# Branch hints, a shorter last wait, a split check and two PSUM banks at the end of a two-block attention kernel

## Chip, cores, metric

The kernel runs on one core of one Trainium2 chip. The metric is the device time of that core in microseconds (us). One execution of each kernel was also recorded by the profiler. Its "span" runs from the first to the last record and is about 1.8 us shorter than the device time of the same execution (853.9 beside 855.72 before the change).

## The reference, cut to what matters

Two cached attention blocks on the same shapes, written side by side into one output of 16 x 32 x 2048. Block A has 32 query heads on 4 K/V heads, block B has 32 K/V heads.

```python
# B = 16 batches, Sq = 32 queries, D = 1024, Sk = 1024 keys, Dh = 128, all bf16
def _A_ref(x, k_cache, v_cache, wq, wo):            # k_cache, v_cache: B x 4 x Sk x Dh
    q = (x @ wq).reshape(B, Sq, 32, Dh).transpose(0, 2, 1, 3)
    k, v = jnp.repeat(k_cache, 8, axis=1), jnp.repeat(v_cache, 8, axis=1)
    p = softmax(einsum("bhqd,bhkd->bhqk", q, k) * Dh ** -0.5)
    o = einsum("bhqk,bhkd->bhqd", p, v)
    return o.transpose(0, 2, 1, 3).reshape(B, Sq, 32 * Dh) @ wo
# _B_ref: the same without the repeat; k_cache, v_cache: B x 32 x Sk x Dh
return jnp.concatenate([a, b], axis=-1)
```

The traffic is almost all loads: 337.6 MB read, of which the K and V of block B are 268 MB, and 2.1 MB written.

## The kernel before, cut to what the argument touches

The kernel holds two programs. The fast one takes exponentials without subtracting a row maximum. It notes every reciprocal of a softmax sum and at its end checks that all lie between 1e-10 and 1e10; the answer becomes a number in SBUF, the flag. The second, "general", program is safe for all inputs and follows behind a branch on that flag. With the inputs of this case the flag is always good, so the branch always jumps over the general program.

```python
def run_engine(self, eng_name, eng, sems):
    for op in self.ops:                      # the engine's own instructions, in scheduled order
        ...
def await_dmas(self, eng, sems):
    for k, c in sorted(self.dma_count.items()):     # all 40 DMA semaphores, two to an instruction
        eng.wait_ge(sems[k], 16 * c)

def whole(name, eng):                        # written once for each of the five engines
    fast.run_engine(name, eng, fast_sems)
    eng.wait_ge(fast_sems[flag_op.eng], flag_op.sig)
    reg = eng.alloc_register("flag_" + name)
    eng.reg_load(reg, flag[0:1, 0:1])
    if name == "sp":
        fast.await_dmas(eng, fast_sems)      # before the branch
    with eng.If_ne(reg, flag_good):
        ...                                  # the general program
```

The fast program is a list of operations with what each reads and writes. A list scheduler orders the operations of all engines by modelled times and adds the semaphores, so a small edit can move instructions far from it. It runs 128 steps. Each step does four heads of one batch of B (a "quad") and a part of A. Tokens come in four groups of 128 (G = 0 to 3). At the end of each group's block the output projection adds into `acc`; in the last block it goes to the staging buffer `ost` and from there to the output:

```python
def oproj(pi, blk, G):                       # pi: 0 for A, 1 for B
    for oh in range(NOH):                    # two halves of 512 columns
        for h0_ in range(0, nh, 2):
            ...                              # matmuls into ps_pj, one PSUM bank for both halves
        a_ap = acc[:, pi, G, oh * OUTW:(oh + 1) * OUTW]
        o_ap = ost[:, oh * OUTW:(oh + 1) * OUTW]
        ...
        else:                                # last block
            pr.add("dve", lambda e: e.tensor_tensor(o_ap, a_ap, ps_pj[:, 0:OUTW], ALU.add),
                   reads=[BK_PJ, ("acc", pi, G, oh)], writes=[BK_PJ, "ost"], name="accF")
    if blk == nblk - 1:                      # one store of 128 x 1024 bf16, 256 KB
        pr.add("sp", lambda e: e.dma_start(out_flat[...], ost[:, :]), reads=["ost"], dma_key=f"out{pi}")

def st_check():                              # the last thing in the program
    # DVE: two scans over all 2*128 reciprocals -> good[P, 2]   (>= 1e-10, <= 1e10)
    # PE:  ones x good -> ps_pj[0, 0:2];  DVE: multiply, multiply, cast -> flag
```

A "PV" below is the product of the probabilities of one quad with V: 32 matmuls. After it come, for each quad, a normalization (DVE), a transpose (PE) and a copy (ACT), and after the last quad of a group the output projection of B.

Of the kernel before, what the change touches and what calls it, by code (L numbers as in the profile page):

```python
# [7 lines left out]
ALU = alu_op_type.AluOpType  # L8
ACTF = mybir.ActivationFunctionType
BF = mybir.dt.bfloat16  # L10
F32 = mybir.dt.float32


RINV_LOW, RINV_HIGH = 1e-10, 1e10
NVB_SLOTS = 3
NKB_SLOTS = 2
LAZY_PER_STEP = 100
LAZY_DELAY = 0
# [40 lines left out]
class Prog:  # L59
# [264 lines left out]
    def sem_names(self):  # L324
        return ["pe", "act", "dve", "pool"] + sorted(self.dma_count.keys())

    def run_engine(self, eng_name, eng, sems):
        for op in self.ops:
            if op.eng != eng_name:
                continue  # L330
            for key, val in op.waits:
                eng.wait_ge(sems[key[1]], val)
            last = op.emit(eng)
            if op.dma_key is not None:
                last.then_inc(sems[op.dma_key], 16)
            elif op.sig is not None:
                last.then_inc(sems[op.eng], 1)

    def await_dmas(self, eng, sems):
        for k, c in sorted(self.dma_count.items()):  # L340
            eng.wait_ge(sems[k], 16 * c)


def emit_programs(nc, stack, fast, general, flag, flag_good):


    def semaphores(pr, prefix):
        return {k: stack.enter_context(nc.semaphore(prefix + k)) for k in pr.sem_names()}

    flag_op = [op for op in fast.ops if op.name == "flag"][0]  # L350
    fast_sems, general_sems = semaphores(fast, "s_"), semaphores(general, "g_")
    meet = stack.enter_context(nc.semaphore("meet"))
    engines = ("sp", "pe", "act", "dve", "pool")

    with nc.Block() as block:

        def whole(name, eng):
            fast.run_engine(name, eng, fast_sems)
            eng.wait_ge(fast_sems[flag_op.eng], flag_op.sig)
            reg = eng.alloc_register("flag_" + name)  # L360
            eng.reg_load(reg, flag[0:1, 0:1])
            if name == "sp":
                fast.await_dmas(eng, fast_sems)
            with eng.If_ne(reg, flag_good):
                eng.drain().then_inc(meet, 1)
                eng.wait_ge(meet, len(engines))
                general.run_engine(name, eng, general_sems)
                if name == "sp":
                    general.await_dmas(eng, general_sems)

        block.sync(lambda e: whole("sp", e))
        block.tensor(lambda e: whole("pe", e))
        block.scalar(lambda e: whole("act", e))
        block.vector(lambda e: whole("dve", e))
        block.gpsimd(lambda e: whole("pool", e))
# [106 lines left out]
def build(nc, pa, pb, out):  # L482
    P = 128
    Bn, Sq, D = pa["x"].shape
    NTOK = Bn * Sq
    assert Sq == 32 and Bn % 4 == 0
    NG = NTOK // P
# [32 lines left out]
    with contextlib.ExitStack() as stack:  # L520
        def sb(name, shape, dt):
            return stack.enter_context(nc.sbuf_tensor(name, shape, dt))

        def ps(name, shape, dt):
            return stack.enter_context(nc.psum_tensor(name, shape, dt))

        ident = sb("ident", [P, P], BF)
        zeros = sb("zeros", [P, P], BF)
        id32 = sb("id32", [P, P], F32)
        z32 = sb("z32", [P, P], F32)  # L530
        stat = sb("stat", [P, 2, 4], F32)
        rinv_all = sb("rinv_all", [P, 2 * NIT], F32)
        chk = sb("chk", [P, 2 * NIT], BF)
        good = sb("good", [P, 2], F32)
        ones = sb("ones", [P, 1], F32)
        xT_sb = sb("xT_sb", [P, 2, DJ, NTOK], BF)
        wq_sb = sb("wq_sb", [P, DJ, WQC], BF)
# [16 lines left out]
        VAp_sb = sb("VAp_sb", [P, 2, NCH, Dh + 2], BF)  # L554
        OA_sb = sb("OA_sb", [P, 2, Dh], BF)
        OB_sb = sb("OB_sb", [P, Dh], BF)
        ost = sb("ost", [P, D], BF)

        ps_s = ps("ps_s", [P, 2, 2, 512], F32)
        ps_kt = ps("ps_kt", [P, 512], F32)  # L560
# [4 lines left out]
        BK_S = [[("bank", 0), ("bank", 1)], [("bank", 2), ("bank", 3)]]  # L565
        BK_KT, BK_PT, BK_O, BK_PJ = ("bank", 4), ("bank", 5), ("bank", 6), ("bank", 7)

        pr.add("pool", lambda g: g.memset(zeros[:], 0.0), writes=["zeros"], name="c0")
        pr.add("pool", lambda g: g.affine_select(ident[:], zeros[:], [[1, P]], ALU.not_equal, 1.0, base=0, channel_multiplier=-1),
               reads=["zeros"], writes=["ident"], name="c1")  # L570
        pr.add("pool", lambda g: g.memset(z32[:], 0.0), writes=["z32"], name="c0")
        pr.add("pool", lambda g: g.affine_select(id32[:], z32[:], [[1, P]], ALU.not_equal, 1.0, base=0, channel_multiplier=-1),
               reads=["z32"], writes=["id32"], name="c1")
        for i in range(2):
            pr.add("pool", lambda g, i=i: g.memset(VAp_sb[:, i, :, Dh:Dh + 1], 1.0), writes=[("VAp", i)], name="c0")

# [118 lines left out]
        def oproj(pi, blk, G):  # L695
# [4 lines left out]
            wo_ = woA_sb if pi == 0 else woB_sb  # L700
            wo_res = "woA" if pi == 0 else "woB"
            lazy_flush(("wo", pi, blk))
            for oh in range(NOH):
                for h0_ in range(0, nh, 2):
                    def e_op(e, oh=oh, h0_=h0_):
                        last = None
                        for hh in range(h0_, h0_ + 2):
                            last = e.matmul(ps_pj[:, 0:OUTW], OT[:, gp, hh, :], wo_[:, hh, oh * OUTW:(oh + 1) * OUTW],  # L708
                                            start=(hh == 0), stop=(hh == nh - 1))
                        return last  # L710
                    pr.add("pe", e_op, reads=[("OT", pi, gp, h0_), ("OT", pi, gp, h0_ + 1), (wo_res, h0_), (wo_res, h0_ + 1)], writes=[BK_PJ],
                           name="oprojA" if pi == 0 else "oprojB",
                           dur=0.434 * OUTW / 512, rtag={(wo_res, h0_): blk, (wo_res, h0_ + 1): blk, ("OTv", pi, gp): (blk, G)})
                a_ap = acc[:, pi, G, oh * OUTW:(oh + 1) * OUTW]
                o_ap = ost[:, oh * OUTW:(oh + 1) * OUTW]
                if nblk == 1:
                    evac(o_ap, ps_pj[:, 0:OUTW], reads=[BK_PJ], writes=[BK_PJ, "ost"], name="o_fin")
                elif blk == 0:
                    pr.add("act", lambda e, a_ap=a_ap: e.copy(a_ap, ps_pj[:, 0:OUTW]), reads=[BK_PJ], writes=[BK_PJ, ("acc", pi, G, oh)], name="acc0")
                elif blk < nblk - 1:  # L720
                    pr.add("dve", lambda e, a_ap=a_ap: e.tensor_tensor(a_ap, a_ap, ps_pj[:, 0:OUTW], ALU.add),  # L721
                           reads=[BK_PJ], writes=[BK_PJ, ("acc", pi, G, oh)], name="acc+")
                else:
                    pr.add("dve", lambda e, a_ap=a_ap, o_ap=o_ap: e.tensor_tensor(o_ap, a_ap, ps_pj[:, 0:OUTW], ALU.add),  # L724
                           reads=[BK_PJ, ("acc", pi, G, oh)], writes=[BK_PJ, "ost"], name="accF")
            if blk == nblk - 1:
                pr.add("sp", lambda e: e.dma_start(out_flat[G * P:(G + 1) * P, cols[pi]:cols[pi] + D], ost[:, :]),
                       reads=["ost"], dma_key=f"out{pi}", name="out_dma", dur=P * D * 2)

        class Quad:  # L730
            pass
# [233 lines left out]
        def st_otr(q, eng="dve"):  # L965
# [5 lines left out]
                 writes=[BK_O] + [("OT", 1, gp, h_) for h_ in range(MS)], name="OT_ev", eng=eng,  # L971
                 rtag={"OTps": q.qid}, wtag={("OTv", 1, gp): (q.m, q.G)} if q.last_of_group else None)

        quadsA = [mk_quadA(t) for t in range(NIT)]
        quadsB = [mk_quadB(t) for t in range(NIT)]
        newA = [t for t in range(NIT) if quadsA[t].kv_new]
# [99 lines left out]
        for t in range(NIT):  # L1076
# [14 lines left out]
            if qB.last_of_group:  # L1091
                oproj(1, qB.m, qB.G)
                if qB.G == NG - 1 and qB.m + 1 < NMSB:
                    wo_loadB(qB.m + 1)
            lazy_pop(LAZY_PER_STEP)
        cur_step[0] = 10 ** 9
        lazy_pop(1000)

        def st_check():
            every = [("rinv_all", 0), ("rinv_all", 1)]  # L1100
            pr.add("pool", lambda g: g.memset(ones[:], 1.0), writes=["ones"], name="c0")
            pr.add("dve", lambda e: e.tensor_scalar(chk[:], rinv_all[:], RINV_LOW, None, ALU.is_ge, ALU.min, accum_out=good[:, 0:1]),
                   reads=every, writes=["chk", ("good", 0)], name="check")
            pr.add("dve", lambda e: e.tensor_scalar(chk[:], rinv_all[:], RINV_HIGH, None, ALU.is_le, ALU.min, accum_out=good[:, 1:2]),
                   reads=every, writes=["chk", ("good", 1)], name="check")
            pr.add("pe", lambda e: e.matmul(ps_pj[0:1, 0:2], ones[:], good[:], start=True, stop=True),
                   reads=["ones", ("good", 0), ("good", 1)], writes=[BK_PJ], name="check")
            pr.add("dve", lambda e: e.tensor_tensor(good[0:1, 0:1], ps_pj[0:1, 0:1], good[0:1, 0:1], ALU.mult),
                   reads=[BK_PJ], writes=[("good", 0)], name="check")
            pr.add("dve", lambda e: e.tensor_tensor(good[0:1, 1:2], ps_pj[0:1, 1:2], good[0:1, 0:1], ALU.mult),  # L1110
                   reads=[BK_PJ, ("good", 0)], writes=[("good", 1)], name="check")
            pr.add("dve", lambda e: e.tensor_copy(flag[:], good[0:1, 1:2]), reads=[("good", 1)], writes=["flag"], name="flag")
            pr.add("pool", lambda g: g.memset(ones[:], 1.0), reads=["flag"], writes=["ones"], name="c0")

        st_check()
        pr = pr.list_schedule()
        pr.finalize()
    general = general_program(nc, pa, pb, out)
    with outer:
        emit_programs(nc, outer, pr, general, flag, P * P)  # L1120


def bass_concat_heads__gqa_block_cached__mha_block_cached__near_ridge_kernel(nc, A_x, A_k_cache, A_v_cache, A_wq, A_wo, B_x, B_k_cache, B_v_cache, B_wq, B_wo, out):
# [30 lines left out]
```

## Time and profile before

| | before |
|---|---|
| device time, median of 6 runs (range) | 855.18 us (853.86 to 856.07) |
| span of the profiled execution | 853.9 us |
| PE busy / granted clock | 85% / 0.977 |
| mean DMA rate | 400 GB/s |

These are lines of the profile's page for the kernel before: the busy share in 40 equal slices of the span, in tenths; PEclk is the TensorE clock that was granted, in tenths of full speed.

```profile
span 853.9 us, 27413 instructions
PE   4999999789979897799997879887999867878885
PEclk9999999999999999999999999999999999999998
DMA  9999999999999999999999999999999999999994
GB/s 353 395 411 400 412 405 409 413 410 377 407 406 405 416 411 412 410 401 415 409 409 411 410 412 406 413 410 414 413 401 411 397 410 413 414 411 411 412 385 158
```

The DMA row is 9 everywhere but in the last slice: the kernel is bound by its loads, and PE, at 6 to 9 tenths apart from the first and the last slice, keeps up with them. The last slice (21 us) is different: the rate falls to 158 GB/s, because the loads end in the middle of it, at 841.56 us, and 12.4 us follow without any. That is the stretch that this change is about.

The timeline of the kernel before, end of the span (start us, busy us, engine, source line, operation, out <- in, count; in brackets the idle time before it and what ended it):

```profile
839.12 0.69 DVE L724 TENSOR_TENSOR ost<-acc,ps_pj 128x512 bf16<-128x512 f32 x1 [2.40 <-DMA out_dram<-ost]
...
841.76 0.63 PE L946 MATMUL ps_o<-VB_sb,PT_sb 128*32 128x128 bf16 x32
...
842.47 0.34 DVE L962 TENSOR_SCALAR OB_sb<-ps_o,rinv_all 128x128 bf16<-128x128 f32 x1
...
843.46 1.04 PE L708 MATMUL ps_pj<-woB_sb,OTB_sb 128*128 128x512 bf16 x4 [0.36 <-ACT OTB_sb L584]
844.70 0.69 DVE L724 TENSOR_TENSOR ost<-acc,ps_pj 128x512 bf16<-128x512 f32 x1 [1.89 <-DMA out_dram<-ost]
...
845.44 1.70 PE L708 MATMUL ps_pj<-woB_sb,OTB_sb 128*128 128x512 bf16 x4 [0.95 <-DVE ost L724]
...
847.18 0.69 DVE L724 TENSOR_TENSOR ost<-acc,ps_pj 128x512 bf16<-128x512 f32 x1 [1.79 <-PE ps_pj L708]
...
847.92 0.19 PE L1106 MATMUL ps_pj<-good,ones 128*1 128x2 f32 x2 [0.78 <-DVE ost L724]
...
848.51 0.14 DVE L1112 CAST flag<-good 1x1 int32<-1x1 f32 x1
```

The chain reads downward: the last PV starts 0.20 us after the last V tile has landed; the projection of B follows at 843.46. Its second half uses the same bank as the first, so its matmuls (845.44) wait for the add of the first half (844.70), and they take 1.70 us instead of 1.04. The windows view gives a granted clock of 0.92 for 844 to 846 us and 0.50 for 846 to 848. The last add ends at 847.87, the flag is ready at 848.65.

The branch, by the source line of its instruction (engine, operation, count, duration ns min/median/max, first and last start us):

```profile
L364 ACTq COMPARE_BRANCH  x1: 45/45/45, 849.5 to 849.5; - x1
L364 POOLq COMPARE_BRANCH  x1: 45/45/45, 849.5 to 849.5; - x1
L364 DVEq COMPARE_BRANCH  x1: 72/72/72, 849.5 to 849.5; - x1
L364 PEldq COMPARE_BRANCH  x1: 4047/4047/4047, 849.5 to 849.5; - x1
L364 SPq COMPARE_BRANCH  x1: 50/50/50, 850.7 to 850.7; - x1
```

The compare-and-branch of TensorE alone takes 4047 ns. SyncE branches about 1.2 us after the others, as it first passes twenty wait instructions. The raw records of the end, shortened (start us, duration us; a drain is the instruction with which an engine ends its part, before the engines meet):

```
848.68 - 848.70  0.73 to 0.81   all five engines: load of the flag into a register
849.45 ... 850.62               SyncE: twenty wait instructions, one every 0.061
849.46  0.045                   ScalarE: compare and branch       851.93  its drain
849.53  0.072                   VectorE: compare and branch       852.47  its drain
849.54  4.047                   TensorE: compare and branch       853.64  its drain
849.95                          the last store has landed
850.55  1.505                   a packet of 16384 bytes on an instruction queue
850.69  0.050                   SyncE: compare and branch         853.53  its drain
853.75 to 853.94                the engines meet; end of the span
```

From the last add to the end are 6.07 us. The store needs only 2.08 of them; the rest goes into branches and into the time from a branch to the next instruction (2.4 us on ScalarE, 2.9 on VectorE, 2.8 on SyncE).

### The profile page before, as it was taken

How to read it: one execution, taken by the hardware profiler on the slowest of the kernel's cores; microseconds unless marked ns; L12 is line 12 of the kernel's file. 1: busy time of each engine (PE TensorE's matmuls, PEld its weight loads, DVE VectorE, ACT ScalarE, POOL GpSimd, SP SyncE). 2: the span in 40 equal slices, each digit the busy share in tenths (PEclk: the TensorE clock that was granted, in tenths of full speed). 3: DMA queues.
4: the chain of work that ended last, by engine and by line, in shares of the span. 5: the costliest groups of instructions: out<-in, count | busy, mean ns of one | idle time of the engine just before them, and what ended most of it. 6: DMA issues, size and time to landing. Idle time of an engine off the chain costs nothing.

```text
span 853.9 us, 27413 instructions
## 1 busy us (share of the span) xinstructions
PE 726.1 (85%) x12098; PEld 434.9 (51%) x12098; DVE 545.3 (64%) x1115; ACT 447.1 (52%) x981; POOL 67.9 (8%) x76
## 2 busy tenths in 40 slices
PE   4999999789979897799997879887999867878885
PEld 2556655446545454455554445544555544545552
DVE  0755676567756677467774757675766755766673
ACT  2456666456645464445654445654565554556451
POOL 0000100100000000000000000000000000000000
PEclk9999999999999999999999999999999999999998
DMA  9999999999999999999999999999999999999994
GB/s 353 395 411 400 412 405 409 413 410 377 407 406 405 416 411 412 410 401 415 409 409 411 410 412 406 413 410 414 413 401 411 397 410 413 414 411 411 412 385 158
DMA packets 126845, 341.59 MB, mean 400 GB/s; under 512 B 9984, under 2 KB 9984, under 8 KB 110336
## 3 DMA queue, kind: packets, MB, share of 16 engines
q1 hardware_dynamic: 126720, 339.78, 100.7%
q8 instruction: 96, 1.57, 0.7%
q14 instruction: 29, 0.24, 0.1%
HBM read 337.64 MB, written 2.10 MB: 398 GB/s over the span
## 4 chain that ended last, share of the span: by engine, by line
DMA 49%; PE 29%; DVE 12%; SPq 5%; issue 3%; ACT 1%; POOL 0%; DVEq 0%; POOLq 0%
DMA KB_sb<-in_B_k_cache_dram 29%; DVE KBt_sb L819 10%; PE ps_pj L654 8%; PE ps_s L854 5%; DMA VB_sb<-in_B_v_cache_dram 5%; DMA KA_sb<-in_A_k_cache_dram 5%; PE ps_pj L708 4%; DMA VA_sb<-in_A_v_cache_dram 3%; PE ps_kt L912 3%; DMA wq_sb<-in_B_wq_dram 3%; PE ps_o L946 2%; SPq L799 2%; PE ps_pt L896 2%; PE ps_s L837 2%; DMA woB_sb<-in_B_wo_dram 1%
## 5 line engine op out<-in xcount | busy, mean ns | idle before, releaser
L819 DVE STREAM_TRANSPOSE KBt_sb<-KB_sb 128x1024 f32<-128x1024 f32 x256 | 306.2, 1226 | 75.8 <-DMA KB_sb<-in_B_k_cache_dram 67.8
L877 ACT ACTIVATE P_sb<-ps_s 128x512 bf16<-128x512 f32 x256 | 151.9, 599 | 88.3 <-PE ps_s L854 64.2
L869 ACT ACTIVATE PTA_sb<-ps_s 128x1024 bf16<-128x1024 f32 x128 | 131.3, 1026 | 89.8 <-PE ps_s L837 72.0
L854 PE MATMUL ps_s<-KBt_sb,QB_sb 32*32 32x512 bf16 x4096 | 144.4, 389 | 11.0 <-ACT P_sb L877 6.1
L584 ACT COPY PT_sb<-ps_pt 128x512 f32<-128x512 f32 x128 | 75.0, 586 | 122.3 <-PE ps_o L946 111.0
L654 PE MATMUL ps_pj<-xT_sb,wq_sb 128*128 128x512 bf16 x448 | 122.6, 392 | 10.7 <-DMA wq_sb<-in_B_wq_dram 3.7
L793 POOL COPY VAp_sb<-VA_sb 128x1024 bf16<-128x1024 bf16 x64 | 66.6, 1040 | 757.5 <-DMA VA_sb<-in_A_v_cache_dram 725.4
L946 PE MATMUL ps_o<-VB_sb,PT_sb 128*32 128x128 bf16 x4096 | 82.7, 223 | 35.4 <-DMA VB_sb<-in_B_v_cache_dram 21.2
L896 PE MATMUL ps_pt<-id,P_sb 128*128 128x128 f32 x512 | 99.2, 302 | 6.9 <-ACT P_sb L877 6.0
L946 PEld LDWEIGHTS ps_o<-VB_sb,PT_sb 128*32 128x32 bf16 x4096 | 61.2, 98 | 70.0 <-issue 66.1
L896 PEld LDWEIGHTS ps_pt<-id,P_sb 128*128 128x128 f32 x512 | 79.8, 206 | 27.3 <-ACT P_sb L877 9.6
L837 PE MATMUL ps_s<-QT_sb,KTA_sb 128*128 128x256 bf16 x512 | 83.1, 273 | 6.4 <-ACT PTA_sb L869 2.9
L912 PE MATMUL ps_kt<-VAp_sb,PTA_sb 128*128 128x129 bf16 x1024 | 77.8, 224 | 6.9 <-POOL VAp_sb L793 4.7
L854 PEld LDWEIGHTS ps_s<-KBt_sb,QB_sb 32*32 32x32 bf16 x4096 | 48.6, 89 | 65.7 <-issue 12.2
L962 DVE TENSOR_SCALAR OB_sb<-ps_o,rinv_all 128x128 bf16<-128x128 f32 x128 | 43.9, 343 | 59.4 <-PE ps_o L946 58.6
L912 PEld LDWEIGHTS ps_kt<-VAp_sb,PTA_sb 128*128 128x128 bf16 x1024 | 65.7, 99 | 31.6 <-POOL VAp_sb L793 14.0
L708 PE MATMUL ps_pj<-woB_sb,OTB_sb 128*128 128x512 bf16 x256 | 71.0, 384 | 10.0 <-DMA woB_sb<-in_B_wo_dram 3.8
L708 PE MATMUL ps_pj<-woA_sb,OTA_sb 128*128 128x512 bf16 x256 | 66.6, 385 | 7.9 <-DVE ost L724 3.5
L654 PEld LDWEIGHTS ps_pj<-xT_sb,wq_sb 128*128 128x128 bf16 x448 | 42.2, 109 | 45.9 <-DMA wq_sb<-in_B_wq_dram 6.3
L837 PEld LDWEIGHTS ps_s<-QT_sb,KTA_sb 128*128 128x128 bf16 x512 | 44.8, 98 | 30.4 <-ACT PTA_sb L869 7.1
L882 DVE TENSOR_TENSOR stat<-stat 64x1 f32<-64x1 f32 x256 | 41.9, 164 | 22.5 <-ACT P_sb L877 14.3
L721 DVE TENSOR_TENSOR acc<-acc,ps_pj 128x512 f32<-128x512 f32 x64 | 43.1, 674 | 20.4 <-PE ps_pj L708 19.1
(49 smaller groups left out, 504.8 us busy)
## 6 DMA issues: line engine op xcount, KB each, us to landing
KB_sb<-in_B_k_cache_dram SPq DMA_DIRECT2D x128, 1024.0 KB, 8.9
VB_sb<-in_B_v_cache_dram SPq DMA_DIRECT2D x256, 512.0 KB, 10.1
KA_sb<-in_A_k_cache_dram SPq DMA_DIRECT2D x64, 256.0 KB, 10.2
VA_sb<-in_A_v_cache_dram SPq DMA_DIRECT2D x64, 256.0 KB, 8.6
wq_sb<-in_B_wq_dram SPq DMA_DIRECT2D x16, 512.0 KB, 10.7
woB_sb<-in_B_wo_dram SPq DMA_DIRECT2D x32, 256.0 KB, 10.7
woA_sb<-in_A_wo_dram SPq DMA_DIRECT2D x32, 256.0 KB, 8.6
wq_sb<-in_A_wq_dram SPq DMA_DIRECT2D x12, 512.0 KB, 10.4
```

What stands on the lines that cost most here:

```text
L584: pr.add("act", lambda e: e.copy(dst_ap, src_ap), reads=reads, writes=writes, name=name + "@act", wtag=wtag, rtag=rtag)
L654: last = e.matmul(ps_pj[:, 0:NTOK], pick(src, j), xT_sb[:, pi, j, :], start=(j == 0), stop=(j == DJ - 1))
L708: last = e.matmul(ps_pj[:, 0:OUTW], OT[:, gp, hh, :], wo_[:, hh, oh * OUTW:(oh + 1) * OUTW], start=(hh == 0), stop=(hh == nh - 1))
L793: pr.add("pool", lambda g: g.tensor_copy(VAp_sb[:, sl, :, 0:Dh], VA_sb[:, :, :]), reads=["VA"], writes=[("VAp", sl)], name="VAp_cp", rtag= ...
L819: pr.add("dve", lambda e: e.transpose(KBt_sb[:, sl, t_, :].bitcast(F32).rearrange("p (s r i) -> p s r i", r=2, i=32), KB_sb[:, rs, t_, :]. ...
L837: last = e.matmul(ps_s[:, sbf, c2, i * 2 * P:(i + 1) * 2 * P], KTA_sb[:, sl, c * P:(c + 1) * P], qt, start=True, stop=True)
L854: last = e.matmul(ps_s[32 * cg:32 * cg + 32, sbf, g, :].rearrange("p (sh cl j) -> p sh cl j", sh=4, cl=4), lhsT, kt[32 * a:32 * a + 32, g, ...
L869: pr.add("act", lambda e: e.activation(dst, src, ACTF.Exp, scale=scale), writes=BK_S[sbf] + [("PTA", q.half)], name="expA", rtag={("Sv", s ...
L877: pr.add("act", lambda e, src=src, dst=dst, g=g: e.activation(dst, src, ACTF.Exp, scale=scale, accum_out=st[:, g:g + 1]), writes=[BK_S[sbf ...
L896: last = e.transpose(ps_pt32[:, m * P:(m + 1) * P], p32[:, m:Sk // 2:NPK], id32[:])
L912: last = e.matmul(ps_kt[:, qh * OA0:qh * OA0 + Dh + 1], PTA_sb[:, h, c, qh * P:(qh + 1) * P], VAp_sb[:, sl, 4 * h + c, 0:Dh + 1], start=(h ...
L946: last = e.matmul(ps_o[32 * a:32 * a + 32, 0:Dh], PT_pairs[:, c // 2, 32 * (a ^ (c // 4 * 2)):32 * (a ^ (c // 4 * 2)) + 32, c % 2], VB_sb[ ...
```

## The change

Its intent: cut the end of the kernel. Five things come together.

1. Each engine marks a branch hint a hundred or more of its own operations before the branch (270 on SyncE, ScalarE and VectorE, 120 groups of matmuls on TensorE, 300 on GpSimd), and the branch refers to it. The hint is an instruction of its own, BRANCH_PREFETCH_HINT in the trace.
2. SyncE waits, after its branch, for the semaphores of the output stores alone.
3. The check is split: the first 120 columns are scanned eight steps before the end, the last 8 at the end; four accumulating matmuls count the good ones into one number, so that two VectorE multiplications go.
4. In the last block the two halves of an output projection use two PSUM banks. The staging buffer becomes two buffers, and the stores of the last group are issued half by half.
5. Not written in the diff: from about the middle of the kernel the list scheduler orders instructions differently.

```diff
 def whole(name, eng):
-    fast.run_engine(name, eng, fast_sems)
+    hints = []
+    fast.run_engine(name, eng, fast_sems, (ahead[name], lambda: hints.append(eng.mark_branch_hint_location())))
     eng.wait_ge(fast_sems[flag_op.eng], flag_op.sig)
     reg = eng.alloc_register("flag_" + name)
     eng.reg_load(reg, flag[0:1, 0:1])
-    if name == "sp":
-        fast.await_dmas(eng, fast_sems)
-    with eng.If_ne(reg, flag_good):
+    again, after = "again_" + name, "after_" + name
+    eng.br_ne(reg, flag_good, on_true=again, on_false=after).branch_hint(hints[0])
+    with nc.body(again, valid_engines=[eng.engine]):
         ...                                          # the general program
+        eng.br(after)
+    nc.switch_bb(after)
+    if name == "sp":
+        fast.await_dmas(eng, fast_sems, stored)      # only keys that start with "out"
 ...
-        ost = sb("ost", [P, D], BF)
+        ost = sb("ost", [P, 2, D], BF)               # room from zeros and z32, now inside PT_sb
 ...
+            final = blk == nblk - 1
+            ob = (2 * G + pi) % 2
             for oh in range(NOH):
+                ps_a, bk = (ps_kt, BK_KT) if final and oh % 2 == 1 else (ps_pj, BK_PJ)
 ...
-                o_ap = ost[:, oh * OUTW:(oh + 1) * OUTW]
+                o_ap = ost[:, ob, oh * OUTW:(oh + 1) * OUTW]
 ...
-                           reads=[BK_PJ, ("acc", pi, G, oh)], writes=[BK_PJ, "ost"], name="accF")
+                           reads=[bk, ("acc", pi, G, oh)], writes=[bk, ("ost", ob, oh)], name="accF")
+                    if G == NG - 1:                  # one store of 128 KB for each half
+                        pr.add("sp", ... e.dma_start(out_flat[...], ost[:, ob, oh * OUTW:(oh + 1) * OUTW]), ...)
 ...                                                  # check: two scans at t = 120, two at the end
-            pr.add("pe", lambda e: e.matmul(ps_pj[0:1, 0:2], ones[:], good[:], start=True, stop=True), ...)
-            ...                                      # two DVE multiplications
+                for k_ in range(4):
+                    last = e.matmul(ps_kt[0:1, 448:449], ones[:], good[:, k_:k_ + 1], start=(k_ == 0), stop=(k_ == 3))
```

Note `ob = (2 * G + pi) % 2`: it equals `pi`. The two buffers are therefore one for A and one for B, and two groups of the same block still share one.

## The prediction

> **What bounds the kernel now.** Loads. By the page, DMA is 90% or more busy in 39 of 40 slices (mean 400 GB/s); PE is 85% busy at a granted clock of 0.977. From the DMA issues and landings, a transfer is always outstanding from 0.7 us until the last V tile lands at 841.56 us. Only what comes after that landing, or bytes moved behind it, can be saved.
>
> **The tail before (timeline of the last 15 us, raw instruction records).** The last PV starts at 841.76, output projection B at 843.46. Its halves share one PSUM bank: 1.04 us of matmuls, an add (0.69) that waits for the A store, 1.71 us of matmuls, partly at half clock; the last add ends at 847.87. Then check matmul, three tiny VectorE steps, flag ready 848.65; every engine loads the flag (0.73 to 0.81 us) and branches. TensorE's compare-and-branch lasts 4.05 us (849.54 to 853.58). SyncE first passes twenty wait instructions (849.45 to 850.65), branches at 850.69 and reaches its drain only at 853.53. The last store had landed at 849.95. End 853.94: 6.07 us after the last add.
>
> **What the change does.**
> 1. Branch hints. [...] instruction-queue packets follow the branches of 4.05 and 2.8 us. I expect hinted branches of about 0.1 us.
> 2. SyncE waits for the stores' semaphores only, after its branch: about three instructions for twenty, 1.2 us to 0.2, overlapped.
> 3. Check: scans move earlier; two of three VectorE steps go (0.36 us).
> 4. Last halves in two banks, staging buffer doubled, last stores in halves. Saves one add and one bank turn (about 0.7 us) between the projection's start and the last add.
> 5. The list schedule changes from about the middle on. Both group-2 stores (256 KB each) now stand behind the last V load, which so lands about 1.3 us earlier (840.3). But the doubled buffer has one half for A and one for B, so the last A adds wait for the group-2 A store behind it (about 840.9); VectorE works in order, so norm and PV of the last steps wait behind them. Walking this with the durations above: adds to 842.4, norm, transpose, copy to 843.3, PV to 844.0, norm, transpose, copy to 845.0, eight matmuls to 847.1, last add 848.0 (849.0 if half clock falls there again). Items 4 and 5 cancel.
>
> **Sum.** Last add 848.0 to 849.0; store landing 2.05 later, flag and branch inside that time, drain and barrier 0.5: end at 850.5 to 851.5. Saving 2.4 to 3.4 us, nearly all from items 1 and 2.
>
> Predicted: 852.6 us, 8 in 10 between 850.9 and 855.3. Faster by over 2%: 0.005; within 2%: 0.985; slower: 0.01.
>
> **What would show it.** TensorE's and SyncE's compare-and-branch under 0.3 us; SyncE's drain right after the last store lands; end about 2.6 us after the last add; last V landing near 840.3; the last A adds idle on the staging store.
>
> **What would make it wrong.** The hints have no effect[...]: then TensorE's 4 us stays, time about 855.4. Or the new order starves the load queue in the middle (1 to 3 us), since loads set the end of everything else; or half-clock stretches fall elsewhere.

The sum came to an end at 850.5 to 851.5, and the branch, put at about 0.1 us, lies inside the 2.05 us of the store (issued at 847.90 and landed at 849.95 in before). "VectorE works in order" shows in the profiled pair at the place in question: in after the normalization of the step before last starts at 841.86, behind the two adds (840.66 and 841.26) and 0.81 us after its PV has ended (841.05); in before the last one, with no add to wait behind, starts 0.08 us after its PV (842.39 to 842.47).

## The result

| us | before | after |
|---|---|---|
| device time, median of 6 (range) | 855.18 (853.86 to 856.07) | 853.01 (852.5 to 854.27) |
| last V tile landed | 841.56 | 839.91 |
| last PV starts | 841.76 | 842.85 |
| projection of B, first weight load | 843.45 | 844.52 |
| last add ends | 847.87 | 848.27 |
| last store landed | 849.95 | 850.15 |
| end of the span | 853.94 | 850.69 |
| from last add to end | 6.07 | 2.42 |

The ratio of after to before is 0.9978, with a 95% interval of 0.9965 to 0.9991. The rows below the first are of one profiled execution of each kernel.

The same lines of the page, of the kernel after:

```profile
span 850.7 us, 27284 instructions
PE   3999999799979797788997878887999768787876
PEclk9999999999999999999998999998999999999998
DMA  9999999999999999999999999999999999999995
GB/s 350 377 411 398 410 412 408 410 412 400 413 405 401 414 412 415 408 401 413 403 414 413 409 411 411 414 389 412 411 409 415 411 411 413 411 391 414 403 407 219
```

The body looks the same. The last slice now carries 219 instead of 158 GB/s, as the kernel ends sooner after its loads and its slices are a little shorter.

The timeline of the kernel after, its end:

```profile
839.90 0.59 PE L724 MATMUL ps_kt<-woA_sb,OTA_sb 128*128 128x512 bf16 x2
...
840.42 0.63 PE L964 MATMUL ps_o<-VB_sb,PT_sb 128*32 128x128 bf16 x32
840.66 0.69 DVE L738 TENSOR_TENSOR ost<-acc,ps_pj 128x512 bf16<-128x512 f32 x1 [2.95 <-DMA out_dram<-ost]
...
841.26 0.68 DVE L738 TENSOR_TENSOR ost<-acc,ps_kt 128x512 bf16<-128x512 f32 x1
...
841.86 0.34 DVE L980 TENSOR_SCALAR OB_sb<-ps_o,rinv_all 128x128 bf16<-128x128 f32 x1
...
842.85 0.63 PE L964 MATMUL ps_o<-VB_sb,PT_sb 128*32 128x128 bf16 x32 [0.35 <-ACT OTB_sb L597]
...
844.97 0.87 PE L724 MATMUL ps_kt<-woB_sb,OTB_sb 128*128 128x512 bf16 x2
...
846.48 1.06 PE L724 MATMUL ps_kt<-woB_sb,OTB_sb 128*128 128x512 bf16 x2
...
846.73 0.69 DVE L738 TENSOR_TENSOR ost<-acc,ps_pj 128x512 bf16<-128x512 f32 x1 [2.85 <-PE ps_pj L724]
847.58 0.69 DVE L738 TENSOR_TENSOR ost<-acc,ps_kt 128x512 bf16<-128x512 f32 x1 [0.17 <-PE ps_kt L724]
...
848.32 0.34 PE L1004 MATMUL ps_kt<-good,ones 128*1 128x1 f32 x8 [0.78 <-DVE ost L738]
848.70 0.15 DVE L1007 CAST flag<-ps_kt 1x1 int32<-1x1 f32 x1 [0.43 <-PE ps_kt L1004]
```

Two things are to be seen. The last PV (842.85) starts 2.94 us after the last V tile landed (839.91), not 0.20: VectorE's adds of block A waited for a store from the same staging buffer (2.95 us of idle time, ended by that DMA; the matmuls of the first half ended at 840.06 and the store landed at 840.56, so the store alone held them for about 0.6 us) and ran at 840.66 and 841.26, and the normalization of the step before came behind them (841.86). And in the end the add of the first half (846.73) and the matmuls of the second (846.48) overlap, as they are in two banks. The pair at 846.48 ran at half clock (1.06 us for two matmuls; the windows view gives 0.50 from 846 us on).

The branch of the kernel after:

```profile
L369 ACTq COMPARE_BRANCH  x1: 68/68/68, 849.6 to 849.6; - x1
L369 SPq COMPARE_BRANCH  x1: 75/75/75, 849.6 to 849.6; - x1
L369 POOLq COMPARE_BRANCH  x1: 59/59/59, 849.6 to 849.6; - x1
L369 DVEq COMPARE_BRANCH  x1: 84/84/84, 849.6 to 849.6; - x1
L369 PEldq COMPARE_BRANCH  x1: 412/412/412, 849.6 to 849.6; - x1
```

TensorE: 412 ns in place of 4047. The drains follow at 850.03 (ScalarE), 850.07 (TensorE), 850.18 (VectorE), and SyncE's at 850.47, after three waits in place of twenty, the last of which passes at 850.22, just after the last store has landed (850.15). So the last add came 0.4 us later than before, and the kernel still ended 3.25 us earlier in the profiled pair (2.2 us in the medians).

### The profile page after: what moved, and what is told of

Its sections match the earlier page's. It is cut to its first block, busy times and chain, and to the rows that moved or that the text cites. A ratio compares the mean times of both kernels' runs of the same rounds, so it can differ in the third digit from the quotient of the medians.

```text
span 850.7 us, 27284 instructions
## 1 busy us (share of the span) xinstructions
PE 713.5 (84%) x11974; PEld 435.7 (51%) x12104; DVE 546.6 (64%) x1117; ACT 447.0 (53%) x981; POOL 68.0 (8%) x76
## 4 chain that ended last, share of the span: by engine, by line
DMA 52%; PE 24%; DVE 17%; SPq 4%; issue 2%; ACT 1%; POOL 0%; DVEq 0%; POOLq 0%
DMA KB_sb<-in_B_k_cache_dram 33%; DVE KBt_sb L837 13%; PE ps_pj L667 8%; DMA VA_sb<-in_A_v_cache_dram 5%; PE ps_s L872 4%; DMA VB_sb<-in_B_v_cache_dram 3%; DMA wq_sb<-in_B_wq_dram 3%; PE ps_pj L724 3%; PE ps_kt L930 3%; DMA wq_sb<-in_A_wq_dram 2%; PE ps_o L964 2%; PE ps_pt L914 2%; SPq L817 2%; PE ps_s L855 1%; DMA woB_sb<-in_B_wo_dram 1%
## 5 line engine op out<-in xcount | busy, mean ns | idle before, releaser
L667 PE MATMUL ps_pj<-xT_sb,wq_sb 128*128 128x512 bf16 x404 | 115.3, 396 | 16.7 <-DMA wq_sb<-in_B_wq_dram 4.4
L914 PE MATMUL ps_pt<-id,P_sb 128*128 128x128 f32 x512 | 101.4, 301 | 11.4 <-ACT P_sb L895 8.4
L724 PE MATMUL ps_pj<-woB_sb,OTB_sb 128*128 128x512 bf16 x193 | 58.3, 388 | 9.0 <-ACT OTB_sb L597 2.6
L900 DVE TENSOR_TENSOR stat<-stat 64x1 f32<-64x1 f32 x256 | 44.8, 175 | 23.7 <-ACT P_sb L895 15.7
L724 PE MATMUL ps_pj<-woA_sb,OTA_sb 128*128 128x512 bf16 x198 | 51.5, 379 | 6.9 <-DMA woA_sb<-in_A_wo_dram 2.3
```

What stands on the lines that cost most here:

```text
L667: last = e.matmul(ps_pj[:, 0:NTOK], pick(src, j), xT_sb[:, pi, j, :], start=(j == 0), stop=(j == DJ - 1))
L724: last = e.matmul(ps_a[:, 0:OUTW], OT[:, gp, hh, :], wo_[:, hh, oh * OUTW:(oh + 1) * OUTW], start=(hh == 0), stop=(hh == nh - 1))
L914: last = e.transpose(ps_pt32[:, m * P:(m + 1) * P], p32[:, m:Sk // 2:NPK], id32[:])
```

## Experiments

Theory after the result: hints and short wait together are the whole gain, about 3.5 us from the last add to the end. The new order with its earlier loads and the staging wait cancel each other. Rivals: the short wait alone does it; or the earlier end of the loads does it and the branch was never on the path; or the staging buffer costs more than the early loads give.

All kernels below gave correct results. "Lag" is the time from the landing of the last V tile to the end of the last add; "tail" the time from there to the end of the span. Both are from the one profiled execution of each kernel.

| kernel | median us (range; runs) | ratio to before [95%] | V landed | lag | tail |
|---|---|---|---|---|---|
| before | 855.18 (853.86 to 856.07; 6) | 1 | 841.56 | 6.31 | 6.07 |
| after | 853.01 (852.5 to 854.27; 6) | 0.9978 [0.9965, 0.9991] | 839.91 | 8.36 | 2.42 |
| e1_nohint | 856.31 (854.15 to 858.49; 6) | 1.0016 [0.9994, 1.0038] | 841.18 | 7.52 | 5.86 |
| e2_end_only | 851.35 (850.35 to 852.5; 6) | 0.9958 [0.9939, 0.9977] | 841.44 | 5.59 | 2.58 |
| e3_waits_only | 854.93 (853.62 to 859.57; 6) | 1.0017 [0.9992, 1.0042] | 840.25 | 5.60 | 6.00 |
| e4_stage | 851.81 (850.1 to 855.37; 6) | 0.9976 [0.9953, 0.9999] | 839.16 | 6.74 | 2.39 |
| e5_onebank | 854.12 (851.7 to 856.59; 6) | 0.9992 [0.9976, 1.0008] | 845.46 | 6.19 | 3.13 |
| e6_joined | 850.80 (850.45 to 853.22; 5) | 0.9955 [0.9942, 0.9967] | 843.00 | 6.03 | 2.39 |
| e7_hint_near | 855.81 (853.58 to 857.01; 6) | 1.0013 [0.9998, 1.0028] | 839.95 | 8.25 | 5.51 |
| e8_check | 853.17 (852.25 to 854.92; 5) | 0.9988 [0.9973, 1.0002] | 840.95 | 5.96 | 3.53 |
| f1_changed | 852.44 (851.68 to 853.75; 6) | 0.9977 [0.996, 0.9993] | 839.97 | 7.41 | 2.43 |
| f2_end_only | 851.96 (851.3 to 852.02; 5) | 0.9967 [0.9949, 0.9984] | 841.72 | 5.60 | 2.57 |
| f3_stage | 851.13 (850.19 to 852.88; 6) | 0.9959 [0.9941, 0.9977] | 840.08 | 7.64 | 2.39 |
| f4_order | 849.68 (849.13 to 850.44; 6) | 0.9942 [0.9926, 0.9958] | 840.05 | 5.91 | 2.39 |

e1 to e4 ran on one chip beside 11 runs of before (median 854.89), e5 to e8 on a second beside 11 others (854.70), f1 to f4 on a third beside 11 more (854.57). No two of these kernels differ by as much as 1%, so the argument rests on the ratios within a round and on the traces. Two cautions on reading: the last V tile landed up to 1.8 us apart in profiles with one order of instructions (839.95 in e7, 841.72 in f2), so that small steps can hardly be read from total times; and PE fell to half clock ahead of the last add in some profiled executions (before, after, e7, f3) and not in the others, which is worth about 0.9 us of lag: 8.36 us in after, and 7.41 us in f1, the same kernel at full clock.

### Hints and waits: e1, e2, e3

e1_nohint is the changed kernel with the hints taken out:

```diff
-fast.run_engine(name, eng, fast_sems, (ahead[name], lambda: hints.append(eng.mark_branch_hint_location())))
+fast.run_engine(name, eng, fast_sems)
-eng.br_ne(reg, flag_good, on_true=again, on_false=after).branch_hint(hints[0])
+eng.br_ne(reg, flag_good, on_true=again, on_false=after)
```

> The changed kernel with the branch hints taken out, the rest as it is. Theory (the hints are most of the gain): TensorE's compare-and-branch goes back to about 4 us (0.41 in the changed kernel), it then ends about 853.6 us after the start and the span is 3 us longer than the changed kernel's; time about 855.5 to 856, same as the kernel before within 0.1%. Rival (the shorter list of waits on SyncE and the new order made the gain, the hints nothing): within 0.5 us of the changed kernel, about 853.

Measured: 856.31 us, ratio 1.0016. The tail is 5.86 us again. The branch of TensorE in this kernel, in the form shown above:

```profile
L369 SPq COMPARE_BRANCH  x1: 50/50/50, 850.0 to 850.0; - x1
...
L369 PEldq COMPARE_BRANCH  x1: 4127/4127/4127, 850.1 to 850.1; - x1
```

SyncE branches at 850.0, among the first, since its waits come later; TensorE's branch takes 4.13 us, and the kernel ends behind it. Without hints nothing of the gain is left.

e2_end_only is the other side: the kernel before with items 1 and 2 alone (hints, and the stores-only wait after the branch), every other instruction in the old order.

```diff
 # before.py, in whole() and run_engine() exactly as in the diff of the change; nothing else
+    stored = [k for k in sorted(fast.dma_count) if k.startswith("out")]
+    ahead = {"sp": 270, "pe": 120, "act": 270, "dve": 270, "pool": 300}
```

> The kernel before with the hints and the stores-only wait of SyncE alone; order, check, staging and banks as before. Theory (items 1 and 2 are the gain, items 3 to 5 cancel in the tail): about 2.6 us from the last add plus the longer check (0.3 us) to the end, so a span 3.2 us shorter than before, time about 851.7 to 852.3, at or below the changed kernel's 853.0. Rival (two banks, check and new order are worth about 1 us more): 853 to 854, above the changed kernel.

Measured: 851.35 us, ratio 0.9958; tail 2.58 us. The two items alone give at least as much as the whole change. TensorE's branch in this kernel:

```profile
L368 PEldq COMPARE_BRANCH  x1: 412/412/412, 848.7 to 848.7; - x1
```

e3_waits_only is e2 without its hints:

```diff
-eng.br_ne(reg, flag_good, on_true=again, on_false=after).branch_hint(hints[0])
+eng.br_ne(reg, flag_good, on_true=again, on_false=after)
```

> As the last, but without the hints: the kernel before with SyncE's stores-only wait alone. Theory: TensorE's branch of 4 us ends after everything SyncE does, so nothing is gained: within 0.3 us of the kernel before, end still about 6 us after the last add. Rival (SyncE's twenty waits are on the path): 1 us faster.

Measured: 854.93 us, ratio 1.0017; tail 6.00 us, TensorE's branch 3.97 us. The seventeen waits saved gain nothing by themselves: they ran while TensorE's branch was under way. Whether the hints alone, with the long wait kept, would have gained all was not run. In before, SyncE's own branch started 1.15 us after the last of the others, and what that costs with a hint was not measured.

### The staging buffer: e4

e4_stage is the changed kernel with the last group staged in `acc` of group 0, which is dead by then. Every engine's instructions stay in the same order; only the wait of A's last adds for the group-2 store goes.

```diff
-o_ap = ost[:, ob, oh * OUTW:(oh + 1) * OUTW]
+if G == NG - 1:
+    o_ap, o_res = acc[:, pi, 0, oh * OUTW:oh * OUTW + OUTW // 2].bitcast(BF), ("acc", pi, 0, oh)
+else:
+    o_ap, o_res = ost[:, ob, oh * OUTW:(oh + 1) * OUTW], ("ost", ob, oh)
```

> The changed kernel with the last group's output staged in a dead part of the accumulator, so its adds wait for no earlier store; the order of instructions is identical on every engine. Theory: the first last-group A add starts when its matmuls end (about 840.1 instead of 840.66), but the second half's add and PV of the step before last bound the norm behind it, so only about 0.35 us is gained in the tail; time within 0.5 us of the changed kernel. Rival (the wait for the store held up the whole tail): the last add 1 us or more earlier, time about 852.

Measured: 851.81 us, ratio 0.9976, not to be told from after by its time. In the profile the wait is gone, but the last PV still starts 2.27 us (841.43 after 839.16) after the last V tile, against 2.94 with the wait. So the wait was worth about 0.7 us, and most of the delay has another cause. The timeline of after suggests one: all 16 matmuls of A's last projection (to 840.4 us) stand ahead of the PV of the step before last (840.42) on TensorE. f4, below, tests it.

### One bank: e5

e5_onebank is the changed kernel with both halves in one bank again.

```diff
-ps_a, bk = (ps_kt, BK_KT) if final and oh % 2 == 1 else (ps_pj, BK_PJ)
+ps_a, bk = (ps_kt, BK_KT) if False else (ps_pj, BK_PJ)
```

> The changed kernel with all last-group halves back in one PSUM bank; hints, short wait, split check, two-part staging buffer and half stores stay. The scheduler then puts half of A's last projection behind the PV of the step before last, as in the kernel before. Theory (the changed kernel's order in the tail, with all of A's last 16 matmuls ahead of that PV, costs about 2.8 us between the last V landing and the last PV, and the two banks give back 1.0 us at the end): last PV starts within 0.4 us of the last V landing (2.9 in the changed kernel), the last add ends about 5.6 us after that landing at full clock (7.5 without hints at full clock), and the time is about 852.0, 0.5 to 1.5 us below the changed kernel. Rival (the order does not matter, run-to-run spread of the load stream made the difference): lag from V landing to last add 7 us or more, time 853 or above.

Measured: 854.12 us, ratio 0.9992: a miss, about 2 us slower than expected. The last PV starts 0.87 us after the last V tile and the last add ends 6.19 us after it: nearer to the theory (under 0.4 and 5.6) than to the rival (7 or more), but neither is met. The profiled execution, the slowest of the six, lost its time elsewhere: its last V tile landed at 845.46, 5.5 us later than in after, with a transfer outstanding all the time. The slowest stretch, by windows (columns: stretch, its length, busy us of PE, PEld, DVE, ACT, POOL with counts, granted clock, DMA share, GB/s):

```profile
472.00:474.00 2.00, 1.86 (x40) 1.04 (x38) 2.00 (x3) 1.10 (x2) 0.00 (x0) 1.00 0.84 322
474.00:476.00 2.00, 1.50 (x35) 0.60 (x35) 1.87 (x5) 1.18 (x3) 0.84 (x1) 1.00 0.70 191
```

At 474 to 476 us the rate falls to 191 GB/s, under half of the mean of 400. The kernel has two banks or one only in the last block, hundreds of us later, but the edit also changes the scheduled order. The trace shows what came before the slow stretch: TensorE ran at half clock from 457.9 to 471.55 us (6.8 us long near there in after, 3.4 in before), and no load was issued between 465.74 and 473.95. By the two rates shown against 410 GB/s this stretch cost about 1.5 us (an estimate), so most of the 5.5 us lies elsewhere. Whether the order or the run's chance brought the long half clock is open. The effect of the banks has to be read at the place itself, from the start of B's projection to the last add, among executions that ran at full clock there: 3.76 us with one bank (e2: 843.27 to 847.03), 2.79 with two (e4: 843.11 to 845.90; f1: 844.59 to 847.38). Two banks save 0.97 us. (In the profiled pair of before and after, both in part at half clock, the same stretch from the first weight load took 4.42 and 3.75 us: 0.67 saved.)

### The good parts joined: e6

e6_joined is e2 with the split check, the last group staged in the dead part of `acc` and stored by halves, and two banks in the very last projection only; the staging buffer for the other groups stays single. Its edit also gives the stores of those groups another priority in the list scheduler (`prio=0`), which is not cut out below.

```diff
+ps_a, bk = (ps_kt, BK_KT) if (end and pi == 1) and oh % 2 == 1 else (ps_pj, BK_PJ)
+if end:
+    o_ap, o_res = acc[:, pi, 0, oh * OUTW:oh * OUTW + OUTW // 2].bitcast(BF), ("acc", pi, 0, oh)
+else:
+    o_ap, o_res = ost[:, oh * OUTW:(oh + 1) * OUTW], "ost"
```

> A joined version: hints, short wait and split check; two banks for B's last group only; the last group staged in a dead part of the accumulator, stored in halves; one staging buffer for the rest. Theory: last V landing to last PV under 0.4 us as in the kernel before, projection B to last add 2.8 us as in the changed kernel, last add about 4.7 us after the V landing, end 2.4 us later: time about 850.3, about 1 us below the run with hints and short wait alone (851.35). Rival (nothing left but the hints): 851.3 or above.

Measured: 850.80 us, ratio 0.9955, about as fast as e2 (0.9958). Its profiled execution was its slowest (853.22 us), with a last V tile at 843.00, so its profile says little on the gain of the joined parts. Two things can be read in it. From the start of B's projection to the last add it took 2.79 us, as two banks should. But the last PV started 1.53 us after its V tile, where under 0.4 had been expected, so the lag was 6.03 us and not 4.7. The further 1 us below e2 did not come.

### Hints close to the branch: e7

e7_hint_near is e2 with each hint only eight operations before the branch.

```diff
-ahead = {"sp": 270, "pe": 120, "act": 270, "dve": 270, "pool": 300}
+ahead = {"sp": 8, "pe": 8, "act": 8, "dve": 8, "pool": 8}
```

> Hints and short wait on the kernel before as in the earlier run, but every hint stands 8 of the program's operations before the end instead of 120 to 300; that is about 4 us before the branch on TensorE. Theory A[...]: TensorE's branch takes 1 us or less, time within 0.5 us of 851.35. Theory B[...]: TensorE's branch again near 4 us, time about 854.9 as before.

Measured: 855.81 us, ratio 1.0013; tail 5.51 us. (Its lag is long as A's last store took 4.2 us, from 840.97 to 845.20, and B's add waited for it; half clock followed. Beside that store a packet of 16384 bytes moved on an instruction queue, from 841.91 to 843.70, 1.7 us after TensorE's hint; see e8.) The engines differ, and neither theory holds for all of them. (A is that so near a hint works, B that it does not.) From the records:

| engine | hint, instructions ahead | hint, us ahead of its branch | outcome |
|---|---|---|---|
| TensorE | 76 | 9.7 | branch 0.49 us: worked |
| VectorE | 13 | 10.8 | drain 0.6 us after the branch: worked |
| ScalarE | 15 | 19 | drain only at 853.41: not |
| SyncE | 10 | 26 | next instruction only at 852.52: not |

More time ahead did not help: the two engines with the longest time are the two that failed. No rule follows from four points, and it stays open. What is shown is that two engines without a working hint are enough to lose the gain of the tail, as the program ends with the slowest. In the changed kernel the hints stand 272 (SyncE), 374 (ScalarE), 295 (VectorE), 1212 (TensorE) and 82 (GpSimd) instructions ahead, and those of the first four work. GpSimd's drain followed its branch within 0.2 us in before too, without a hint.

### The check alone: e8

e8_check is e2 with the split check (item 3) added.

```diff
-pr.add("pe", lambda e: e.matmul(ps_pj[0:1, 0:2], ones[:], good[:], start=True, stop=True), ...)
+for k_ in range(4):
+    last = e.matmul(ps_kt[0:1, 448:449], ones[:], good[:, k_:k_ + 1], start=(k_ == 0), stop=(k_ == 3))
 # and: first 120 columns scanned at step 120, last 8 at the end; flag_good 4 * P
```

> Hints and short wait on the kernel before, with the split check too; banks and staging as before. Theory (the flag is ready before the last store has landed, so the check is not on the path): the end stays about 2.6 us after the last add, set by the store's landing, time within 0.7 us of 851.35. Rival (the check's VectorE steps were on the path): about 0.4 us from the last add to the end less, and 1 us less in all.

Measured: 853.17 us, ratio 0.9988: a miss, 1.8 us slower than e2. In its profile the flag is ready at 841.95, five us before the last add ends, since the check no longer shares a bank with the projection. Yet the tail grew to 3.53 us: the last store, 256 KB, took 3.0 us from its issue (846.94) to its landing (849.94), where the same store took 2.05 to 2.06 in before, e2 and others. In e5 the flag was early as well (847.47), and its last store of 128 KB took 2.6 us in place of 1.86 to 1.87. These are the only two kernels whose flag was ready before the last store was issued.

The packets of the traces show what comes with the early flag. In every kernel with far hints, an instruction queue moves a packet of 16384 bytes 1.1 to 1.6 us after the start of TensorE's branch. In after this is at 850.74, when the last store has landed (850.15). In e8 and e5 TensorE branches before the last store is issued, and the packet moves beside the store: 846.83 to 847.91 in e8, 851.56 to 852.73 in e5. Over all fourteen profiles, 44 stores landed after the last V tile. In three of them such a packet overlapped the store's own data, and these are the slow ones: 2.61 us (e5, 128 KB), 3.01 (e8) and 4.23 (e7, both 256 KB). In three more it was in flight when the store was issued, with the last loads still under way: 1.89 (e6), 2.08 (f4) and 2.35 us (e5), all of 128 KB. The other 38 took 1.81 to 1.87 us for 128 KB and 2.02 to 2.06 for 256 KB. In e7, nine of the store's 144 packets, a sixteenth, start only after 843.6, when the instruction packet is about to end (843.70); the others had all started by 842.7. So the instruction packet beside the store is the likely cause; no run moved that packet alone, and how it would slow the store was not shown. It would explain 1 us of e8's miss; the rest lies in the spread of the loads or is open.

### A round for the close ones: f1 to f4

f1_changed is the changed kernel and f2_end_only is e2, both unedited, to compare on one chip.

> The changed kernel once more, on the same chip and in the same rounds as the next three. About 2.0 us below the kernel before (ratio 0.9975 to 0.998).

> Hints and short wait alone, once more, beside the changed kernel. Theory 1 (what the tail before the last add gained and lost cancels, as predicted): within 0.6 us of the changed kernel. Theory 2 (the new order in the tail costs about 1.5 us net, as the first pair of runs suggests): 1 to 2 us below it, ratio to before about 0.996.

Measured: 852.44 and 851.96 us, ratios 0.9977 and 0.9967. The 1.7 us by which e2 seemed better than after shrinks to 0.5, inside the intervals. The two profiles show why they come out alike: in f1 the last V tile landed 1.75 us earlier (839.97 against 841.72), and the lag was 1.81 us longer (7.41 against 5.60). This is the cancelling that was predicted. One pair could be chance, as landings spread by up to 1.8 us; but the six profiles with the order of before (before, e2, e3, e7, f2 and, but for the check, e8) have a median landing of 841.2, the six of the changed kernel and its staged forms (after, e1, e4, f1, f3, f4) one of 840.0. The ranges overlap.

f3_stage is e4, again unedited; f4_order is f3 with one dependency more: the second half of A's last projection may not be scheduled before the PV of the step before last.

```diff
+# PV of quad t also writes ("pvdone", t); A's last projection, oh == 1, last group:
+reads=[...] + [("pvdone", NIT - 2)]
```

> The changed kernel with the last group staged in dead accumulator rows, once more, as the base of the next. Theory: 0.3 to 0.5 us below the changed kernel; last V landing to last add 6.7 us at full clock.

> The staged version with one more dependency: the second half of A's last projection (8 matmuls) may start only after the PV of the step before last. The order then differs from the staged version in the last 19 TensorE operations and the last 9 VectorE operations, nowhere else, so the load stream is the same. Theory (the cost is that order): last V landing to last PV about 1.1 us (2.3 in the staged version), to last add about 5.6 us at full clock (6.7), time about 1 us below the staged version, near 850. Rival (the order of the tail is not what costs): lag to the last add above 6.4 us, time within 0.3 us of the staged version.

Measured: 851.13 us (0.9959) and 849.68 us (0.9942). f3 is 1.3 us below f1, where 0.3 to 0.5 had been expected; the intervals overlap, and its lag of 7.64 us had half clock in it. Its timeline, at the three places that matter:

```profile
840.51 0.63 PE L966 MATMUL ps_o<-VB_sb,PT_sb 128*32 128x128 bf16 x32
...
841.39 0.34 DVE L982 TENSOR_SCALAR OB_sb<-ps_o,rinv_all 128x128 bf16<-128x128 f32 x1
...
842.37 0.63 PE L966 MATMUL ps_o<-VB_sb,PT_sb 128*32 128x128 bf16 x32 [0.35 <-ACT OTB_sb L597]
```

f4 differs from f3 only in the order of the last 19 groups of TensorE and the last 9 instructions of VectorE. The timeline of f4, in the form used above:

```profile
838.49 0.59 PE L724 MATMUL ps_pj<-woA_sb,OTA_sb 128*128 128x512 bf16 x2
...
839.01 0.63 PE L966 MATMUL ps_o<-VB_sb,PT_sb 128*32 128x128 bf16 x32
...
839.58 1.04 PE L724 MATMUL ps_kt<-woA_sb,OTA_sb 128*128 128x512 bf16 x4
...
839.77 0.35 DVE L982 TENSOR_SCALAR OB_sb<-ps_o,rinv_all 128x128 bf16<-128x128 f32 x1
...
841.46 0.63 PE L966 MATMUL ps_o<-VB_sb,PT_sb 128*32 128x128 bf16 x32
...
844.67 0.69 DVE L741 TENSOR_TENSOR acc<-acc,ps_pj 128x512 bf16<-128x512 f32 x1 [2.15 <-PE ps_pj L724]
845.28 0.68 DVE L741 TENSOR_TENSOR acc<-acc,ps_kt 128x512 bf16<-128x512 f32 x1
```

The adds of the last group now write into `acc`, which serves as staging. The PV of the step before last (839.01) comes before eight of A's matmuls (839.58 on), and its normalization follows at 839.77, where it came at 841.39 in f3 and 841.86 in after. The last PV starts at 841.46, 1.41 us after its V tile (840.05), against 2.29 in f3 and 2.94 in after and f1. The last add ends 5.91 us after the landing; the kernel before needed 6.31 and e2 5.59. So f4 keeps the earlier loads, the two banks and the hints. It beats both kernels: 0.9942 [0.9926, 0.9958] against before, and its slowest run (850.44) is faster than the fastest of after (852.5) and of f1 (851.68). Against f3 its median is 1.45 us better, but the two intervals overlap slightly.

## Why the prediction was right

The prediction (852.6 us, 850.9 to 855.3) met 853.01 us. Point by point:

- **Bound by loads, only the tail can be saved: held.** All that the kernels differ by is when the last V tile lands, the lag and the tail.
- **Item 1, hints: right, one figure missed.** TensorE's branch fell from 4.05 to 0.41 us; about 0.1, and under 0.3 in what it would show, had been predicted. e1 shows that the whole gain hangs on it. What the traces show beside the branch is packets on a queue that the profile's page lists as an instruction queue (q8: 96 packets, 1.57 MB in before). One of 16384 bytes moves at 850.55 us in before, while TensorE stands in its branch. Such a packet starts 1.0 us into TensorE's branch in before, e1 and e3, the three kernels without hints. With hints none moves while the branch lasts (after, e2), and in e7, with a hint close to the end, one moves at 841.91, 1.7 us after TensorE's hint and 8 us before its branch. These are times side by side: what the branch waits for, and how a hint shortens it, was not shown.
- **Item 2, short wait: right.** Three waits, ending at 850.22 us, in the shadow of the last store. e3 shows that alone it gains nothing.
- **Item 3, check: right that it is off the path, size wrong.** From the last add to the flag took 0.78 us before (847.87 to 848.65) and 0.58 after (848.27 to 848.85), a saving of 0.20 and not 0.36: the four accumulating matmuls take 0.34 us in place of 0.19. The store lands last in either case.
- **Item 4, two banks: right.** Predicted 0.7 us from the start of the projection to the last add; measured 0.67 in the profiled pair, where half clock fell into both, and 0.97 at full clock.
- **Item 5, order and staging: the sum right, the mechanism in part wrong.** The last V tile was predicted at 840.3 and landed at 839.91; the store that the adds wait for was predicted at 840.9 and landed at 840.56; the last add was predicted for 848.0, or 849.0 at half clock, and ended at 848.27 with half clock. "Items 4 and 5 cancel" held: f1 and f2 differ by 0.5 us. But the prediction said "norm and PV of the last steps wait behind them", meaning VectorE's adds. That is what the trace of after shows, and yet it is not the main cause: of the 2.94 us between the last V tile and its PV, taking the wait away (e4, f3) removes 0.65 to 0.67, and moving eight matmuls of A (f4) another 0.88. Taken in this sequence, the order was the larger term, and the prediction did not name it. (f4 also reorders VectorE's last nine instructions, so the 0.88 belongs to both engines; the new order with the store's wait kept was not run.) The last 1.41 us were not tested; in the old order (e2) they are 0.14. The trace of f4 shows TensorE busy for 2.41 of the 2.46 us from 839.00 to the last PV, eight matmuls of A among it: when V lands earlier, TensorE still has this work in front of it.
- **The sum.** An end at 850.5 to 851.5 was predicted, 850.69 came. The saving in the profiled pair, 3.25 us, lies within the predicted 2.4 to 3.4; that of the medians, 2.2 us, is just under it. That the sum came out so well is in part luck: the last add was expected 0.7 us later for a tail with half clock (849.0) than it came (848.27), and the delay before the last PV had the size that the prediction's walk gives (about 3.1 us, from V at 840.3 to the start of the PV; 2.94 came), though taking its reason away removes less than a quarter of it.

What stays open: the long half clock before the slow stretch in e5, most of its late landing, whether the instruction packet alone made the stores of e5, e7 and e8 slow, the rest of e8's miss, and when a near hint works.

## What to carry to other kernels

When a loop bound by loads has been tuned, look at what comes after the last landing, and take every engine's branch and drain by itself: a branch over code that never runs cost 4 us here, and the slowest engine set the end. Look also at when packets move on the instruction queues: the three stores whose data met one were the slowest, up to 4.2 us in place of about 2. A delay with a plain releaser in the trace (here a wait for a store) can have a second cause just behind it; take the first away and see how much of the delay is left. After any change to a list-scheduled kernel compare the last instructions of each engine: one added dependency, which moved eight matmuls behind a critical PV and reordered VectorE to match, gave about as much (0.88 us) as the two banks (0.97 us).

## What the runs show of branches, stores and the clock

- **Branches.** Four things, with their numbers here:
  - The cost without a hint: 3.97 to 4.13 us on TensorE, inside the branch instruction itself (before, e1, e3). On ScalarE, VectorE and SyncE it is the time between a branch of 0.05 to 0.07 us and the next instruction: 2.4 to 2.9 us in before, 2.7 to 3.3 us in e1.
  - What a hint gives: TensorE's branch from 4.05 to 0.41 us, the tail from 5.86 (e1) to 2.42 us.
  - How far ahead it stood. The hints of the changed kernel that worked stood 272 to 374 instructions ahead on SyncE, ScalarE and VectorE and 1212 on TensorE (44 to 373 us before the branch). Those that stood 10 and 15 ahead on SyncE and ScalarE failed (e7), and 13 and 76 ahead on VectorE and TensorE worked there. How near one may stand was not shown.
  - Loading the flag, one value in SBUF, into a register took 730 to 810 ns in the kernel before and 640 to 670 ns in the kernel after.
- **Short stores.** The stores here are issued by SyncE and at the end of the kernel took 2.02 to 2.06 us for 256 KB and 1.81 to 1.87 us for 128 KB, data included. The three whose data met a packet of 16384 instruction bytes took 2.61 (e5), 3.01 (e8) and 4.23 us (e7).
- **Half clock.** The clock records of before and after hold 18 stretches at half clock that end inside the span: 16 of them lasted 3.41 us, two (in after) 6.83. TensorE was not idle ahead of the four stretches looked at: it was busy 1.61 of 3.4 us before the stretch that begins at 845.7 us in before, 1.44 ahead of 845.1 in after (these two last beyond the end of the span), and 1.35 and 1.93 ahead of two stretches in the body of before (722.8 and 763.8 us). In f1 it was busy 1.87 us from 842.2 to 845.6, and full clock followed (1.00 from 845.6 to 849.0). What brings the half clock was not shown.
